# Twelve-token chunks and earlier first products at the head of a fused attention and MoE kernel

## The chip, the cores and the metric

The kernel runs on one core of a Trainium2 chip. The metric is device time in microseconds (us) of one execution. A profiled execution shows a span some 1.8 us shorter than its device time.

## The reference, cut to what matters

```python
# q, k, v: (4, 6080, 256) float32; w_in (256, 2048); w_out (2048, 256)
qn = q / (norm(q, axis=1) + 1e-6);  kn = k / (norm(k, axis=1) + 1e-6)   # norms over the 6080 tokens
s = kn.transpose(0, 2, 1) @ qn / tau                                    # 256 x 256 for each batch
a = softmax(s, axis=-1)
x = v @ a
out = gelu_tanh(x @ w_in) @ w_out
```

The kernel multiplies `a` into `w_in` first (`aw`), so that each block of 512 tokens of v needs one product with `aw` (`hp`), a gelu (`g`) and one product with `w_out` (`yp`). Batch 0's `aw` must exist before that loop begins. The attention of batch 1 is worked on inside the loop of batch 0, and so on.

## The kernel before: the parts that matter

The head, batch 0 (cut):

```python
first_chunks = chunks_of([6, 6, 5, 6, 6, 6, 4, 4, 2, 2], 2)   # tokens per partition; chunk 2 also takes the last 64 tokens
...
for n, ch in enumerate(first_chunks):        # cast q and k to bf16 (DVE), square (ACT), G += k.T q (PE), column sums (PE)
    ...
    stage_chunk(n + 4)                       # next loads, into a free buffer of four
...
for fs in range(D // 512):                   # w_in in four pieces, cast by the load: GpSimd's queue
    nc.gpsimd.dma_start(out=win_bf[:, :, fs * 512 : fs * 512 + 512], in_=...)
load_v(1)
...                                          # w_out in two halves
load_qk(1, 0)                                # batch 1's first chunk of q and k, same queue
load_v(2)
...
T = turned(Gs)
for jc in range(2):
    nc.scalar.activation(eT[:, jc, :], T[:, jc, :], AF.Exp, scale=r[:, jc : jc + 1])
...                                          # v's first block turned on PE
rsinv = row_sums(eT)
...                                          # eight products eT x w_in, scaled by rsinv into aw
```

The loop, what the argument touches (cut):

```python
def attention_steps(b, aw_next):             # one step between two hp groups
    for n in range(10):
        if n % 5 == 0 and (b, n // 5) not in loaded_of:
            load_qk(b, n // 5)
        ...
        yield
    for n, ch in enumerate(later_chunks):
        load_qk(b, n + 2)                    # two chunks ahead of their use
        ...
for blk in range(n_blocks):
    vT = vT_of.pop(nb)
    turn_v(nb + 2)                           # four DMA transposes on SP, vT <- vb, for block nb + 2
    load_v(nb + 3)
    ...
```

## Time and profile before

757.6 us, the median of three runs. The stages of the profiled execution, read from the order of time (starts in us):

| last cast of q, k | root (norms) | T | first hp of the loop | first hp of block 2 | span |
|---|---|---|---|---|---|
| 35.44 | 37.19 | 38.77 | 41.52 | 67.00 | 755.3 |

In the order of time of PE's products (start, length, line, what; in brackets the idle time before it and what is named as ending it) around the start of block 2:

```profile
66.24 0.38 PE L141 MATMUL G<-qkb 128*128 128x256 bf16 x2
67.00 1.02 PE L536 MATMUL hp<-vT,aw 128*128 128x512 bf16 x4 [0.38 <-ACT g L540]
```

PE waits 0.38 us here. The name in brackets is a gelu. But hp also reads vT, and vT of block 2 is written by the transposes that SP issues in this line of its own order of time:

```profile
55.15 10.65 SPq L294 DMA_TRANSPOSE vT<-vb  x8
```

By the landing records of the trace, the fourth of these (the last one for block 2) landed at 66.75, 0.25 us before hp began. The length of an issue in that line is not the time to landing: the fourth was issued at 59.40.

### The profile page before, as it was taken

To read this page: it belongs to the slowest core of one execution; us is meant where nothing else is said; L and a number is where in the kernel's file an instruction comes from. 1 tells how busy PE (TensorE), PEld (TensorE's weight loads), DVE (VectorE), ACT (ScalarE), POOL (GpSimd) and SP (SyncE) were. 2 spreads that over 40 slices of the span, in tenths; PEclk is the share of its full clock that TensorE was granted. 3 is DMA by queue.
4 is the path that set the end of the run, shared out by engine and by line. 5 is a ranking of instruction groups with operands and counts; after the bars stand their busy time and mean duration, and the time that the engine had idled before them with its cause. 6 is when DMAs were issued, how large, how long until landed. Compare 5 with 4: busy or idle time off the path is not lost.

```text
span 755.3 us, 12358 instructions
## 1 busy us (share of the span) xinstructions
PE 738.0 (98%) x5272; PEld 504.6 (67%) x5272; DVE 278.3 (37%) x485; ACT 420.3 (56%) x412; POOL 70.0 (9%) x127
## 2 busy tenths in 40 slices
PE   4899999999999999999999999999999999999998
PEld 3556666667666666666666666666767666666666
DVE  3645545454402545553421455454441011011011
ACT  5775555556455555555555555555545655555552
POOL 0231010001021111001031000100101000000000
PEclk9999999999999999999999999999999999999999
DMA  9999957115149678313449385621512633322111
GB/s 351 357 194 180 189 87 154 53 43 83 43 103 214 133 133 137 65 43 66 101 94 221 80 130 101 125 80 47 82 43 78 111 79 76 69 74 53 41 57 56
DMA packets 80759, 83.59 MB, mean 111 GB/s; under 512 B 55488, under 2 KB 60224, under 8 KB 80704
## 3 DMA queue, kind: packets, MB, share of 16 engines
q0 software_dynamic: 17648, 32.97, 27.0%
q1 hardware_dynamic: 62752, 48.98, 24.6%
q8 instruction: 41, 0.67, 0.4%
q10 hardware_dynamic: 304, 0.85, 0.3%
q14 instruction: 14, 0.11, 0.1%
HBM read 78.91 MB, written 24.90 MB: 137 GB/s over the span
## 4 chain that ended last, share of the span: by engine, by line
PE 95%; DMA 3%; DVE 0%; ACT 0%; SPq 0%; issue 0%; DVEq 0%
PE yp L463 44%; PE hp L536 44%; PE G L141 5%; DMA st<-in_k_dram 3%; PE ps L201 2%; PE cols L153 1%; PE T L179 0%; PE yp L567 0%; PE idle L137 0%; SPq L80 0%; DVE qkb L242 0%; ACT g L540 0%; PE ps L348 0%; ACT eT L328 0%; DVE Gs L171 0%
## 5 line engine op out<-in xcount | busy, mean ns | idle before, releaser
L540 ACT ACTIVATE g<-hp 128x1024 bf16<-128x1024 f32 (+1 forms) x384 | 389.8, 1015 | 308.6 <-PE hp L536 308.5
L463 PE MATMUL yp<-wout_bf,g 128*128 128x256 bf16 x3024 | 392.0, 273 | 0.0
L536 PE MATMUL hp<-vT,aw 128*128 128x512 bf16 (+1 forms) x1536 | 390.8, 377 | 0.4 <-ACT g L540 0.4
L463 PEld LDWEIGHTS <-g 128*128 128x128 bf16 x3024 | 295.9, 98 | 113.4
L536 PEld LDWEIGHTS <-aw 128*128 128x128 bf16 x1536 | 149.9, 98 | 105.0 <-issue 1.3
L480 DVE COPY ysb<-yp 128x512 f32<-128x512 f32 (+1 forms) x95 | 64.9, 683 | 403.1 <-PE yp L463 403.1
L404 DVE TENSOR_TENSOR acc<-acc,sq 128x512 f32<-128x512 f32 (+1 forms) x141 | 97.5, 692 | 4.8
L141 PE MATMUL G<-qkb 128*128 128x256 bf16 (+1 forms) x384 | 69.8, 282 | 12.8 <-DVE qkb L242 12.8
L403 DVE TENSOR_TENSOR sq<-qkb 128x512 bf16<-128x512 bf16 (+1 forms) x141 | 58.7, 417 | 0.0
L141 PEld LDWEIGHTS <-qkb 128*128 128x128 bf16 (+1 forms) x384 | 37.8, 101 | 21.5 <-DVE qkb L242 15.0
L280 POOL DMA_DIRECT2D vb<-in_v_dram x47 | 25.5, 544 | 142.7 <-DMA vT<-vb 122.8
L210 DVE TENSOR_SCALAR aw<-ps,rsinv 128x512 bf16<-128x512 f32 x30 | 22.4, 749 | 27.0 <-PE ps L201 26.7
L247 ACT ACTIVATE sqb<-st 128x3072 bf16<-128x3072 f32 (+3 forms) x9 | 20.4, 2287 | 11.6 <-DMA st<-in_k_dram 11.6
L80 POOL DMA_DIRECT2D qkb<-in_q_dram x24 | 13.0, 542 | 148.7 <-PE hp L536 82.4
L242 DVE CAST qkb<-st 128x3072 bf16<-128x3072 f32 (+4 forms) x11 | 14.5, 1326 | 15.4 <-DMA st<-in_k_dram 15.3
L201 PE MATMUL ps<-win_bf,eT 128*128 128x512 bf16 x60 | 17.7, 379 | 0.0
L414 POOL TENSOR_TENSOR r<-r,half 128x4 f32<-128x4 f32 x3 | 3.1, 1044 | 141.7 <-DVE r L413 141.7
L80 POOL DMA_DIRECT2D qkb<-in_k_dram x24 | 13.1, 544 | 4.1 <-DMA qkb<-in_q_dram 2.3
L520 POOL COPY g<-gr 128x1024 bf16<-128x1024 bf16 x2 | 2.1, 1040 | 105.3 <-PE yp L463 105.3
L439 DVE RECIPROCAL den<-den 128x256 f32<-128x256 f32 x6 | 10.5, 1753 | 0.2
L554 POOL COPY gr<-g 128x1024 bf16<-128x1024 bf16 x2 | 2.1, 1036 | 87.6 <-ACT g L540 87.6
L137 PE MATMUL idle<-filler 128*128 128x512 bf16 x36 | 9.5, 391 | 0.0
(65 smaller groups left out, 85.1 us busy)
## 6 DMA issues: line engine op xcount, KB each, us to landing
out_dram<-ysb SPq DMA_DIRECT2D x44, 512.0 KB, 2.9
vb<-in_v_dram POOLq DMA_DIRECT2D x43, 256.0 KB, 8.6
qkb<-in_q_dram POOLq DMA_DIRECT2D x21, 384.0 KB, 6.6
qkb<-in_k_dram POOLq DMA_DIRECT2D x21, 384.0 KB, 8.7
st<-in_q_dram SPq DMA_DIRECT2D x5, 768.0 KB, 9.5
st<-in_k_dram SPq DMA_DIRECT2D x4, 768.0 KB, 11.3
vT<-vb SPq DMA_TRANSPOSE x184, 3.5
out_dram<-ysb SPq DMA_DIRECT2D x4, 384.0 KB, 4.0
```

The source lines that it names most:

```text
L80: engines[x].dma_start(out=dst[:, x, 0:size, :], in_=src[b, s0 * 128 : (s0 + size) * 128, :].rearrange("(p s) c -> p s c", s=size))
L141: nc.tensor.matmul(G[:, ic, :], lhsT=qk[:rows, 1, s, ic * 128 : ic * 128 + 128], rhs=qk[:rows, 0, s, :], start=first and ic == 0, stop=las ...
L201: nc.tensor.matmul(ps, lhsT=eT[:, jc, ic * 128 : ic * 128 + 128], rhs=win_bf[:, jc, fs * 512 : fs * 512 + 512], start=jc == 0, stop=jc == 1)
L210: nc.vector.tensor_scalar_mul(dst, ps, scale)
L247: nc.scalar.activation(sqb[:rows, :, lo:hi], st[:rows, :, lo:hi], AF.Square)
L280: nc.gpsimd.dma_start(out=t[:, 0:n, :], in_=v_rows[r0 : r0 + n * 128, :].rearrange("(p s) c -> p s c", s=n))
L403: nc.vector.tensor_mul(sq[:rows], flat, flat)
L404: nc.vector.tensor_add(acc[:rows], acc[:rows], sq[:rows])
L463: nc.tensor.matmul(yp[:rows, at, :], lhsT=g[:, fc, s * 128 : s * 128 + rows], rhs=wout_bf[:, fc, :], start=fc == 0, stop=fc == FC - 1)
L480: nc.vector.tensor_copy(ysb[:, s0 : s + 1, :], yp[:, 0 : s + 1 - s0, :])
L536: nc.tensor.matmul(hp[:, j, :cols], lhsT=aw[:, cc, fc * 128 : fc * 128 + 128], rhs=vT[:, cc, :cols], start=cc == 0, stop=cc == 1)
L540: nc.scalar.activation(g[:, 2 * i : 2 * i + 2, :cols], hp[:, :, :cols], AF.Gelu_apprx_tanh)
```

## The change

Its intent: load batch 0's first 24 tokens per partition as rows of 12 KB of q and of k alone, each in a whole buffer, with fewer transfers; square the last chunk on ACT alone; turn v's first block while the norms are worked out; begin the first weight products when half of the exponentials are there. On GpSimd's queue the last two pieces of w_in become one, and v's block 2 is asked for ahead of batch 1's first q and k. The core of the diff, cuts marked:

```diff
-    first_chunks = chunks_of([6, 6, 5, 6, 6, 6, 4, 4, 2, 2], 2)
+    first_chunks = chunks_of([12, 12, 5, 6, 4, 4, 2, 2], 2)
 ...
+    def halves(pool, tag, dtype, size, most=SMAX):   # q and k in a tile each where a chunk has over 6 tokens
 ...
-    for fs in range(D // 512):
-        nc.gpsimd.dma_start(out=win_bf[:, :, fs * 512 : fs * 512 + 512], ...)
+    for c0, c1 in ((0, 512), (512, 1024), (1024, D)):
+        nc.gpsimd.dma_start(out=win_bf[:, :, c0:c1], in_=win_v[:, :, c0:c1])
     load_v(1)
 ...
+    load_v(2)
     load_qk(1, 0)
-    load_v(2)
 ...
-    keep_clock(5)
+    ...                                   # the eight transposes of v's first block on PE
+    keep_clock(1, pY, "y")
     T = turned(Gs)
+    keep_clock(1, pY, "y")
 ...
+    first_aw(0, 0)                        # needs the first half of the exponentials only
+    first_aw(1, 0)
     rsinv = row_sums(eT)
+    first_aw(0, 1)
+    first_aw(1, 1)
 ...
```

More of the change, by code (lines that the diff above doesn't have):

```diff
@@ L80, in load_chunk @@
             engines[x].dma_start(
-                out=dst[:, x, 0:size, :],
+                out=dst[x][:, 0:size, :],
                 in_=src[b, s0 * 128 : (s0 + size) * 128, :].rearrange("(p s) c -> p s c", s=size))
@@ L84, in load_chunk @@
             for x, src in enumerate((q, k)):
-                engines[x].dma_start(out=dst[:REM, x, size, :], in_=src[b, S_ALL * 128 : N, :])
+                engines[x].dma_start(out=dst[x][:REM, size, :], in_=src[b, S_ALL * 128 : N, :])
     def slots_of(chunk):
@@ L91 @@
     n_all = S_ALL + 1
-    first_chunks = chunks_of([6, 6, 5, 6, 6, 6, 4, 4, 2, 2], 2)
-    TAIL, SHARED = 6, 8
-    fillers = [0, 0, 5, 5, 6, 7, 4, 3, 1, 0]
+    first_chunks = chunks_of([12, 12, 5, 6, 4, 4, 2, 2], 2)
+    TAIL, SHARED = 4, 6
+    fillers = [0, 0, 5, 7, 4, 3, 1, 0]
     staged = []
+    def halves(pool, tag, dtype, size, most=SMAX):
+        tiles = [pool.tile([128, 2, most, 256], dtype, tag=tag, name=tag)
+                 for _ in range(1 if size <= most else 2)]
+        if len(tiles) == 1:
+            return [tiles[0][:, x] for x in range(2)], tiles[0]
+        return [t.rearrange("p a b c -> p (a b) c") for t in tiles], None
     def stage_chunk(n):
         if n < len(first_chunks):
+            _, size, rem = first_chunks[n]
             if n < SHARED:
-                st = stage.tile([128, 2, SMAX, 256], FP32, tag="st", name="st")
+                st, whole = halves(stage, "st", FP32, size)
             else:
-                st = staged[n - 2][:, :, first_chunks[n - 2][1] + first_chunks[n - 2][2] :, :]
+                _, size, rem = first_chunks[n - 2]
+                whole = staged[n - 2][1][:, :, size + rem :, :]
+                st = [whole[:, x] for x in range(2)]
             load_chunk((nc.sync, nc.scalar if n < 1 else nc.sync), st, 0, first_chunks[n])
-            staged.append(st)
-    for n in range(4):
+            staged.append((st, whole))
+    for n in range(2):
         stage_chunk(n)
@@ L131, with keep_clock @@
     wout_v = moe_w_out.rearrange("(t p) d -> p t d", p=128)
-    def keep_clock(n):
+    def keep_clock(n, pool=pH, tag="h"):
         for _ in range(n):
-            idle = pH.tile([128, 2, 512], FP32, tag="h", name="idle")
-            nc.tensor.matmul(idle[:, 0, :], lhsT=filler[:, 0:128], rhs=filler, start=True, stop=True)
+            idle = pool.tile([128, 2, 512] if pool is pH else [128, 512], FP32, tag=tag, name="idle")
+            nc.tensor.matmul(idle[:, 0, :] if pool is pH else idle, lhsT=filler[:, 0:128], rhs=filler, start=True, stop=True)
     def gram(G, qk, s, rows, first, last):
@@ L142, in gram @@
                 G[:, ic, :],
-                lhsT=qk[:rows, 1, s, ic * 128 : ic * 128 + 128],
-                rhs=qk[:rows, 0, s, :],
+                lhsT=qk[1][:rows, s, ic * 128 : ic * 128 + 128],
+                rhs=qk[0][:rows, s, :],
                 start=first and ic == 0,
@@ L154, in col_sums @@
                 cols[:, m : m + 1],
-                lhsT=x[:, m // 2, m % 2 * 128 : m % 2 * 128 + 128],
+                lhsT=x[m // 2][:, m % 2 * 128 : m % 2 * 128 + 128],
                 rhs=ones,
@@ L220, in sums_of @@
         for m, x in enumerate(parts):
-            col_sums(cols, x, ones_bf[: x.shape[0], :], summed == 0, last and m == len(parts) - 1)
+            col_sums(cols, x, ones_bf[: x[0].shape[0], :], summed == 0, last and m == len(parts) - 1)
             summed += 1
@@ L227, in pairs_of @@
         h = size // 2
-        pair = prp.tile([128, 2, SMAX // 2, 256], BF16, tag="pair", name="pair")
-        nc.vector.tensor_add(pair[:, :, 0:h], sqb[:, :, 0:h], sqb[:, :, h : 2 * h])
-        parts = [pair[:, :, s, :] for s in range(h)]
+        pair, whole = halves(prp, "pair", BF16, h, SMAX // 2)
+        for x in range(2):
+            nc.vector.tensor_add(pair[x][:, 0:h], sqb[x][:, 0:h], sqb[x][:, h : 2 * h])
+        parts = [[y[:, s, :] for y in pair] for s in range(h)]
         if size % 2:
-            parts.append(sqb[:, :, size - 1, :])
+            parts.append([y[:, size - 1, :] for y in sqb])
+        if first_chunks[n][2]:
+            parts.append([y[:REM, size, :] for y in sqb])
         sums_of(parts, False)
@@ L236 @@
     for n, ch in enumerate(first_chunks):
-        st = staged[n]
+        st, whole = staged[n]
         size = ch[1]
-        qkb = qkp.tile([128, 2, SMAX, 256], BF16, tag="qk", name="qkb")
-        sqb = sqp.tile([128, 2, SMAX, 256], BF16, tag="sq", name="sqb")
+        qkb, qk_whole = halves(qkp, "qk", BF16, size)
+        sqb, sq_whole = halves(sqp, "sq", BF16, size)
         for lo, hi, rows in [(0, size, 128)] + ([(size, size + 1, REM)] if ch[2] else []):
-            nc.vector.tensor_copy(qkb[:rows, :, lo:hi], st[:rows, :, lo:hi])
-            if n >= n_chunks - 2:
-                nc.scalar.activation(sqb[:, 1, lo:hi], st[:, 1, lo:hi], AF.Square)
-                nc.vector.tensor_mul(sqb[:, 0, lo:hi], qkb[:, 0, lo:hi], qkb[:, 0, lo:hi])
-            else:
-                nc.scalar.activation(sqb[:rows, :, lo:hi], st[:rows, :, lo:hi], AF.Square)
+            if whole is None:
+                todo = [(qkb[x][:, lo:hi], sqb[x][:, lo:hi], st[x][:, lo:hi]) for x in range(2)]
+            else:
+                todo = [(y[:rows, :, lo:hi] for y in (qk_whole, sq_whole, whole))]
+            for to, sq, x in todo:
+                nc.vector.tensor_copy(to, x)
+                if n != n_chunks - 2:
+                    nc.scalar.activation(sq, x, AF.Square)
+            if n == n_chunks - 2:
+                nc.scalar.activation(sqb[1][:, lo:hi], st[1][:, lo:hi], AF.Square)
+                nc.vector.tensor_mul(sqb[0][:, lo:hi], qkb[0][:, lo:hi], qkb[0][:, lo:hi])
         keep_clock(fillers[n])
@@ L254 @@
             waiting = None
-        if n < TAIL:
+        if n < 2:
+            pairs_of(n, sqb)
+        elif n < TAIL:
             waiting = (n, sqb)
         else:
-            sums_of([sqb[:rows, :, s, :] for s, rows in slots_of(ch)], n == n_chunks - 1)
-        stage_chunk(n + 4)
+            sums_of([[y[:rows, s, :] for y in sqb] for s, rows in slots_of(ch)], n == n_chunks - 1)
+        for x in ((2, 3) if n == 0 else (4, 5) if n == 1 else (n + 4,)):
+            stage_chunk(x)
         if n == n_chunks - 3:
-            nc.gpsimd.tensor_copy(gate[:, 0:1], st[0:1, 1, 0, 0:1])
+            nc.gpsimd.tensor_copy(gate[:, 0:1], st[1][0:1, 0, 0:1])
     v0 = stage.tile([128, 2, SMAX, 256], FP32, tag="st", name="v0")
@@ L304, in load_qk @@
             t = qkp.tile([128, 2, SMAX, 256], BF16, tag="qk", name="qkb")
-            load_chunk((nc.gpsimd, nc.gpsimd), t, b, later_chunks[n])
-            loaded_of[b, n] = t
-    for fs in range(D // 512):
-        nc.gpsimd.dma_start(out=win_bf[:, :, fs * 512 : fs * 512 + 512],
-                            in_=win_v[:, :, fs * 512 : fs * 512 + 512])
+            views = [t[:, x] for x in range(2)]
+            load_chunk((nc.gpsimd, nc.gpsimd), views, b, later_chunks[n])
+            loaded_of[b, n] = views, t
+    for c0, c1 in ((0, 512), (512, 1024), (1024, D)):
+        nc.gpsimd.dma_start(out=win_bf[:, :, c0:c1], in_=win_v[:, :, c0:c1])
     load_v(1)
@@ L323 @@
     Gs = scaled(G, r)
-    keep_clock(5)
+    vps = []
+    for cc in range(2):
+        p = pH.tile([128, 2, 512], FP32, tag="h", name="vps")[:, 0, :]
+        for s in range(4):
+            nc.tensor.matmul(p[:, s * 128 : s * 128 + 128],
+                             lhsT=v0[:, s, cc * 128 : cc * 128 + 128],
+                             rhs=ident, is_transpose=True)
+        vps.append(p)
+    keep_clock(1, pY, "y")
     T = turned(Gs)
+    keep_clock(1, pY, "y")
+    vT0 = vts.tile([128, 2, 512], BF16, tag="vT", name="vT")
@@ L326 @@
+    nc.vector.tensor_copy(vT0[:, 0, :], vps[0])
     eT = smx.tile([128, 2, 256], BF16, tag="eT", name="eT")
+    aw = awp.tile([128, 2, D], BF16, tag="aw", name="aw")
     for jc in range(2):
         nc.scalar.activation(eT[:, jc, :], T[:, jc, :], AF.Exp, scale=r[:, jc : jc + 1])
-    vT0 = vts.tile([128, 2, 512], BF16, tag="vT", name="vT")
-    for cc in range(2):
-        vps = pH.tile([128, 2, 512], FP32, tag="h", name="vps")[:, 0, :]
-        for s in range(4):
-            nc.tensor.matmul(vps[:, s * 128 : s * 128 + 128],
-                             lhsT=v0[:, s, cc * 128 : cc * 128 + 128],
-                             rhs=ident, is_transpose=True)
-        if cc == 0:
-            nc.vector.tensor_copy(vT0[:, cc, :], vps)
-        else:
-            nc.scalar.activation(vT0[:, cc, :], vps, AF.Copy)
@@ L340 @@
-    rsinv = row_sums(eT)
-    aw = awp.tile([128, 2, D], BF16, tag="aw", name="aw")
-    for lo, pool, tag in ((0, pY, "y"), (256, pA, "a")):
-        for ic in range(2):
-            ps = pool.tile([128, 512], FP32, tag=tag, name="ps")
-            for jc in range(2):
-                nc.tensor.matmul(
-                    ps[:, 0:256],
-                    lhsT=eT[:, jc, ic * 128 : ic * 128 + 128],
-                    rhs=win_bf[:, jc, lo : lo + 256],
-                    start=jc == 0, stop=jc == 1)
-            dst, scale = aw[:, ic, lo : lo + 256], rsinv[:, ic : ic + 1]
-            if lo == 0 and ic == 1:
-                nc.scalar.activation(dst, ps[:, 0:256], AF.Copy, scale=scale)
-            else:
-                nc.vector.tensor_scalar_mul(dst, ps[:, 0:256], scale)
+    nc.scalar.activation(vT0[:, 1, :], vps[1], AF.Copy)
@@ new lines, with first_aw @@
+    firsts = []
+    def first_aw(n, jc, pool=pY, tag="y"):
+        if jc == 0:
+            firsts.append(pool.tile([128, 512], FP32, tag=tag, name="ps"))
+        nc.tensor.matmul(
+            firsts[n][:, 0:256],
+            lhsT=eT[:, jc, n % 2 * 128 : n % 2 * 128 + 128],
+            rhs=win_bf[:, jc, n // 2 * 256 : n // 2 * 256 + 256],
+            start=jc == 0, stop=jc == 1)
+    first_aw(0, 0)
+    first_aw(1, 0)
+    rsinv = row_sums(eT)
+    first_aw(0, 1)
+    first_aw(1, 1)
+    for n in (2, 3):
+        first_aw(n, 0, pA, "a")
+        first_aw(n, 1)
@@ L358 @@
+    for n in range(4):
+        ic, lo = n % 2, n // 2 * 256
+        dst, scale = aw[:, ic, lo : lo + 256], rsinv[:, ic : ic + 1]
+        if n == 1:
+            nc.scalar.activation(dst, firsts[n][:, 0:256], AF.Copy, scale=scale)
+        else:
+            nc.vector.tensor_scalar_mul(dst, firsts[n][:, 0:256], scale)
     nc.scalar.activation(dummy, ones_f, AF.Gelu_apprx_tanh)
@@ L393, in attention_steps @@
             load_qk(b, n + 2)
-            qk = loaded_of.pop((b, n))
+            qk, whole = loaded_of.pop((b, n))
             for s, rows in slots_of(ch):
@@ L397, in attention_steps @@
                 gram(G, qk, s, rows, first, last)
-                flat = qk[:rows, :, s, :]
+                flat = whole[:rows, :, s, :]
                 if first:
@@ L410, in attention_steps @@
         cols = pA.tile([128, 512], FP32, tag="a", name="cols")
-        col_sums(cols, acc, ones_f, True, True)
+        col_sums(cols, [acc[:, x] for x in range(2)], ones_f, True, True)
         r = smx.tile([128, 4], FP32, tag="r", name="r")
```

## The prediction

> **What bounds the kernel now.** I read the page first, then the chain of waits, then the windows of the first 50 us, then the order of time there. The page says that TensorE sets the pace and that the change can only touch the head:
>
> ```profile
> PE 738.0 (98%) x5272; PEld 504.6 (67%) x5272; DVE 278.3 (37%) x485; ACT 420.3 (56%) x412; POOL 70.0 (9%) x127
> PE   4899999999999999999999999999999999999998
> DMA  9999957115149678313449385621512633322111
> PE 95%; DMA 3%; DVE 0%; ACT 0%; SPq 0%; issue 0%; DVEq 0%
> ```
>
> The reader is to see that PE is busy in 38 of 40 slices and that the chain that ended last is PE for 95% and DMA for 3%. One slice is 18.9 us; DMA is at nine tenths in the first two and never so steadily again. From 41.5 us to the end (714 us) the windows show 709.9 us of PE busy, and the waits between 41 and 80 us list one of 0.4 us for PE, those after it none. The change edits only what precedes the loop, plus the order of a few loads at its start. Everything it can win lies in the first 41.5 us, 5.5% of the span.
>
> In that head the loads come first. The windows (columns: stretch and length, busy time of PE, PEld, DVE, ACT, POOL, clock, DMA share, GB/s):
>
> ```profile
> 4.00:6.00 2.00, 0.00 (x0) 0.00 (x0) 0.00 (x0) 0.00 (x0) 0.00 (x0) 1.00 0.99 418
> 14.00:16.00 2.00, 2.00 (x21) 1.35 (x19) 1.86 (x3) 1.87 (x1) 0.00 (x0) 1.00 0.98 356
> 30.00:32.00 2.00, 2.00 (x26) 1.44 (x24) 2.00 (x3) 2.00 (x2) 0.00 (x0) 1.00 1.02 388
> 34.00:36.00 2.00, 2.00 (x31) 1.71 (x30) 1.68 (x3) 1.78 (x3) 2.00 (x4) 1.00 0.71 169
> ```
>
> The reader is to see a DMA share of about 1 from 4 us to 34 us: there is no gap in the loads to close, only a rate to raise. Then the chain in order of time (start, length, what):
>
> ```profile
> 27.60 1.77 DVE qkb L242
> ...
> 36.40 0.46 PE G L141 x4
> 36.85 0.31 PE cols L153 x8
> ...
> 37.19 0.18 ACT r L320
> ...
> 38.14 0.49 DVE Gs L171
> ...
> 38.77 0.75 PE T L179 x4
> ...
> 39.54 0.85 ACT eT L328 x2
> ...
> 40.44 0.23 PE rs L188 x3
> 40.66 0.90 PE ps L348 x8
> 41.56 0.56 PE hp L536 x2
> ```
>
> The last chunk of q and k lands at 35.43; its cast ends at 36.18, just as PE's backlog with fillers runs out (36.22), so landing and backlog are balanced. After that come the column sums, norms, scaling, turning, two exponentials, row sums and eight weight products, each waiting for the last, up to the first product of the loop at 41.52.
>
> **What the Trainium skill says.** "DMA: Bandwidth & Descriptors", section "Why small descriptors are slow (HBM only)", gives a fixed overhead of about 3 cycles per packet inside the DMA engine. The packet records agree in kind: undisturbed packets of 1, 2, 4, 5 and 6 KB took 46, 84, 160, 200 and 234 ns, about 8 ns plus 38 ns per KB. The same page, section "Issuing engines are not separate DMA queues", says that SP, ACT and GpSimd feed the same 16 engines; the trace agrees, the windows stay near 420 GB/s with k on ACT's queue or on SP's. "TensorE: Matmul & The Clock Gate", Part 1, says that an idle PE runs at half rate until about 3.4 us of activity. Here the first 12 G products took 2.74 us and those at 20.39 took 1.48, although the clock line reads 1.00 throughout. "ScalarE: Activation LUTs" states 0.833 ns per element for any function; 128x2048 in 1904 ns against 128x512 in 624 gives 0.833.
>
> **The change part by part.**
>
> *Rows of 12 KB.* The chunks of 6, 6, 5, 6, 6, 6, 4, 4, 2, 2 tokens per partition become 12, 12, 5, 6, 4, 4, 2, 2: four chunks of six turn into two of twelve. Each engine then moves 32 packets of about 8 + 12x38 = 464 ns instead of 64 of 234: 14.98 us become 14.85. At the measured mean of about 238 after 15 us the gain is up to 0.25. Four fewer transfers drop as many 9 ns completion packets on each engine. I choose **0.2 us** earlier landing. It is small because 6 KB rows already run at 16x6144/234 = 420 GB/s.
>
> *Later start of work.* The first chunk pair now lands when 3.1 MB are in, not 1.6: 16 packets of 464 ns in place of 16 of 234, so at about 7.1 + 3.7 = 10.8 us. DVE casts q and k (1.76 each), until 14.4; PE starts there, not at 8.9, and does 24 cold G products in about 5.5 us. ACT squares the four tiles of six (2.76 each) until about 21.9. This is off the path if it has caught up by the last big chunk, which lands at about 27: chunk 2 lands near 21.8, is cast by about 24.8, and ACT is free near 25. It has, by some 2 us. Cost on the path: **0**.
>
> *Buffers.* Both first chunks take all four stage buffers, so chunk 2 is issued when ACT has squared the first q, at 10.8 + 2.76 = 13.6 us; chunk 1's k is in transfer until about 17.6. Chunk 3 goes out at 16.4, chunks 4 and 5 at about 19.2 and 22, while chunk 2 and then chunk 3 run to 21 and 25. The DMA stays fed by 2 us or more each time. Cost: **0**.
>
> *Last chunk's squares.* Before: cast 0.74, then a DVE product of 0.42, ended 36.74, 1.31 us after the landing. Now ACT squares q and k of the last chunk together, 1024 elements: 624 + 512x0.833 = 1.05 us from the landing. G products end about as the squares do, so sums follow some **0.15 us** earlier; the order on PE takes back the rest of the 0.26.
>
> *Transposes of v before T.* The eight (1.04 us) move from the time of the exponentials, where they were free, to the wait for the norms, where five fillers of 1.24 us were. Both places lie beside other work: **0**. They need v's first block by about 36.8.
>
> *First products by halves.* Before, from T's start at 38.77 to the first product of the loop took 2.75 us. Now two of eight weight products run before the second exponential has ended. T 0.75, two exponentials to 1.61 (by the distances above), row sums to 1.87, six products of 0.11 to 2.53; the scaled copy needs 0.05 + 0.17 (reciprocal) + 0.43 after the row sums, also 2.52. The loop starts 2.55 after T: **0.2 us** saved. ACT's second scaled copy still waits behind the v copy (0.60), and ended only 0.11 us after the loop's first product before, so I trim this to 0.15.
>
> *Weights in three pieces, v2 ahead of batch 1.* The last 1 MB of w_in lands as one. Before, waits on its four pieces ended at 40.63, 41.89 and 44.12 (second to fourth). The products of the third piece ran first at 44.12, over 2 us after it was there; now they wait for the whole last MB. Fewer, longer packets bring it in by my estimate at 43.2, PE now asks at about 43.6: no wait, narrowly. Batch 1's first q and k come about 1.4 us later, near 55, and are asked for at 57.67 - 0.5: **0**.
>
> Sum: 0.2 + 0.15 + 0.15 = 0.5 us; fewer instructions and waits at the seams may give 0.2 to 0.3 more. From the median of 757.6 I take **756.9 us**.
>
> **The rivals.** (1) *Nothing moves*: the slowest DMA engine sets each landing. The records show an instruction fetch of 16 KB that took 1105 ns at 24.58 us; the last 2 KB packets ended at 34.88 on one engine, while the middle ones started the last round near 33.6. If that engine lags more, the 0.2 us vanish: 757.2 to 757.6. If the fetch falls after the loads, up to 1.1 us more are won: 755.8. (2) *A wait on w_in or on v takes the place of the products*: margins of 0.4 us and less. It costs 0.3 to 0.6 us and ends level, 757.4. (3) *The loads run dry* because all buffers sit in two chunks: ACT's squares would have to be over 2 us later than worked out; each us of gap is a us of time, 758 to 759. Against it speaks that ACT was 2.4 us idle and more per chunk before. (4) *PE comes late out of its cold start*: 5 us later, with 48 products at once. If it is still behind at 27 us, 0.5 to 1 us are lost. (5) *The loop slides otherwise*: other DMA timing changes waits of PE; it has only 0.4 us of waits there, so little to win and little seen to lose.
>
> **Range and chances.** The runs before span 757.37 to 758.07, so 0.35 us either way is noise. Best case, 1.1 us from the fetch and 0.8 of the sum: 755.7. Worst likely case, rival 2 or 4 with no gain from the rows: 758.1. Range 755.7 to 758.1. A 2% change is 15.2 us, over a third of the whole head; no part reaches 2 us. Chances: faster 0.005, same 0.99, slower 0.005.
>
> **What would show it right or wrong.** Rows: packets of 12288 bytes near 464 ns, DMA share near 1 from 4 to 34 us, last landing at 35.1 to 35.3. Start: first cast near 10.8, PE from 14.4, but no wait of PE longer than before after the chunk of six. Squares: under 1.65 us from the last landing to the root, 1.76 before. Products: 2.6 us from T to the loop's first product, 2.75 before, and the loop at about 41.0. A wait of the first products or of T for v or w_in would show rival 2; a DMA share well below 1 between 14 and 26 us rival 3. The prediction is wrong if the loop starts on time and the span still moves by over 1.5 us, for then the loop itself, 714 us of PE, has changed.

## The result, and the profile after

Median 758.0 us (757.31 to 758.32, six runs); the kernel before, in the same rounds, 757.59 (757.25 to 758.07). The ratio is 1.0003, 95% interval 0.999 to 1.0016. Here and below a ratio is the mean time of one kernel's fast runs over that of the other's of the same rounds, so not quite the ratio of the medians quoted. The page of the kernel after, the lines that answer to those of before:

```profile
PE 730.0 (97%) x5175; PEld 503.6 (67%) x5262; DVE 277.7 (37%) x486; ACT 420.4 (56%) x412; POOL 69.2 (9%) x126
DMA  8999957225139778313549377721512633322111
PE 90%; issue 5%; DMA 3%; POOL 1%; SPq 0%; ACT 0%; DVE 0%; POOLq 0%; ACTq 0%
PE yp L500 43%; PE hp L573 41%; PE G L153 4%; DMA vb<-in_v_dram 2%; DMA vT<-vb 2%; PE ps L213 1%; SPq L318 0%; POOL win_bf L334 0%; PE cols L165 0%; PE yp L604 0%; POOL wout_bf L337 0%; PE T L191 0%; ACT g L577 0%; POOL vb L304 0%; POOL filler L129 0%
```

(PE's smaller count is mostly records missing from the trace: 1457 hp products are recorded, 1536 weight loads of them.) The chain's DMA share is again 3%, but it is other DMA: before it was k's load in the head, now it is a block of v and its transposes. The chain in order of time (start, length, what) shows where they stand:

```profile
37.79 14.19 DMA vb<-in_v_dram
...
55.91 11.91 DMA vT<-vb
67.82 0.14 issue
67.95 1.02 PE hp L573 x4
```

The reader is to see that nothing of the head's computing is on this chain. The path runs from the issue of v's block 2 at 37.79 over its landing at 51.98 and four transposes to the first hp of block 2. It is not free of the head's loads: GpSimd asks for w_in only when the k of the third-last chunk is there, and in all fourteen profiles it did so 0.17 to 0.18 us after that landing. In the kernel after that was 0.26 us earlier than before (32.58, not 32.84), and the transposes still landed 1.07 us later. The waits of PE from 41 us to the end (total, times, longest):

```profile
PE hp L573 <- DMA vT<-vb: 1.2, 1, 1.2
PE ps L213 <- DMA win_bf<-in_moe_w_in_dram: 0.5, 1, 0.5
PE hp L573 <- DVE aw L394: 0.2, 1, 0.2
```

Two new waits: one for w_in's last 1 MB, one for the transposes. Stage by stage:

| start, us | last cast | root | T | first hp | third piece's products | first hp of block 2 | span |
|---|---|---|---|---|---|---|---|
| before | 35.44 | 37.19 | 38.77 | 41.52 | 44.12 | 67.00 | 755.3 |
| after | 35.22 | 36.83 | 38.16 | 40.91 | 44.21 | 67.95 | 756.2 |

The head won 0.61 us and the loop began at 40.91. All of it was gone by 44.2: the last 1 MB of w_in landed at 44.17, and the products that read it came 3.30 us after the first hp instead of 2.60. At block 2 another 0.86 us were lost. From block 2 on nothing differs: from its first gelu to the end of the span there are 687.2 us in the kernel before, 687.1 in the kernel after, and one or the other in each variant below.

### The profile page after: what moved, and what is told of

Its sections match the earlier page's. It is cut to its first block, busy times and chain, and to the rows that moved or that the text cites. A ratio compares the mean times of both kernels' runs of the same rounds, so it can differ in the third digit from the quotient of the medians.

```text
span 756.2 us, 12239 instructions
## 1 busy us (share of the span) xinstructions
PE 730.0 (97%) x5175; PEld 503.6 (67%) x5262; DVE 277.7 (37%) x486; ACT 420.4 (56%) x412; POOL 69.2 (9%) x126
## 3 DMA queue, kind: packets, MB, share of 16 engines
q1 hardware_dynamic: 62176, 48.20, 24.3%
## 4 chain that ended last, share of the span: by engine, by line
PE 90%; issue 5%; DMA 3%; POOL 1%; SPq 0%; ACT 0%; DVE 0%; POOLq 0%; ACTq 0%
PE yp L500 43%; PE hp L573 41%; PE G L153 4%; DMA vb<-in_v_dram 2%; DMA vT<-vb 2%; PE ps L213 1%; SPq L318 0%; POOL win_bf L334 0%; PE cols L165 0%; PE yp L604 0%; POOL wout_bf L337 0%; PE T L191 0%; ACT g L577 0%; POOL vb L304 0%; POOL filler L129 0%
## 5 line engine op out<-in xcount | busy, mean ns | idle before, releaser
L573 PE MATMUL hp<-vT,aw 128*128 128x512 bf16 (+1 forms) x1457 | 385.0, 377 | 5.4 <-DMA vT<-vb 1.2
L153 PE MATMUL G<-qkb 128*128 128x256 bf16 (+1 forms) x288 | 55.0, 273 | 0.0
L153 PEld LDWEIGHTS <-qkb 128*128 128x128 bf16 (+1 forms) x288 | 27.9, 98 | 3.8 <-issue 0.6
L153 PE MATMUL G<-qk 128*128 128x256 bf16 (+1 forms) x96 | 14.2, 307 | 15.5 <-DVE qk L262 15.4
L264 ACT ACTIVATE sq<-st 128x3072 bf16<-128x3072 f32 (+4 forms) x10 | 21.2, 2160 | 11.8 <-DMA st<-in_q_dram 8.4
L153 PEld LDWEIGHTS <-qk 128*128 128x128 bf16 (+1 forms) x96 | 10.1, 110 | 19.4 <-DVE qk L262 16.8
L262 DVE CAST qk<-st 128x3072 bf16<-128x3072 f32 (+4 forms) x11 | 14.3, 1323 | 13.9 <-DMA st<-in_q_dram 10.1
L213 PE MATMUL ps<-win_bf,eT 128*128 128x512 bf16 x54 | 16.4, 379 | 0.5 <-DMA win_bf<-in_moe_w_in_dram 0.5
## 6 DMA issues: line engine op xcount, KB each, us to landing
st<-in_q_dram SPq DMA_DIRECT2D x2, 1536.0 KB, 11.9
```

The source lines that it names most:

```text
L153: nc.tensor.matmul(G[:, ic, :], lhsT=qk[1][:rows, s, ic * 128 : ic * 128 + 128], rhs=qk[0][:rows, s, :], start=first and ic == 0, stop=las ...
L213: nc.tensor.matmul(ps, lhsT=eT[:, jc, ic * 128 : ic * 128 + 128], rhs=win_bf[:, jc, fs * 512 : fs * 512 + 512], start=jc == 0, stop=jc == 1)
L264: nc.scalar.activation(sq, x, AF.Square)
L573: nc.tensor.matmul(hp[:, j, :cols], lhsT=aw[:, cc, fc * 128 : fc * 128 + 128], rhs=vT[:, cc, :cols], start=cc == 0, stop=cc == 1)
```

## The experiments

**Theory.** The first hp of block 2 waits for the transposes of v's block 2. They share the DMA engines with a stream of loads on GpSimd's queue (w_in, w_out, batch 1's q and k, blocks of v) that is busy without a break from 35 us on, and they land only when that stream pauses. This pins the rest of the program, already in the kernel before. **Rivals**: the wait for w_in alone is the loss; the transposes are slow of themselves; the head's gain was luck. In each diff below, "late third chunk" stands for

```diff
-            load_qk(b, n + 2)
+            for m in ((), (2, 3))[n] if b == 1 and n < 2 else (n + 2,):
+                load_qk(b, m)
```

so that batch 1's third chunk is asked for at 64.8 to 66.4 us in the profiles, not at 53.5 to 55.6. It is used only after the first two chunks.

### What pins the loop

First four runs, on one chip; the kernel before beside them had a median of 757.51 (756.92 to 757.75).

**a_pieces4**: after, with w_in in four pieces.

```diff
-    for c0, c1 in ((0, 512), (512, 1024), (1024, D)):
+    for c0, c1 in ((0, 512), (512, 1024), (1024, 1536), (1536, D)):
```

> Kernel after, w_in's last 1 MB again as two pieces. Theory (stream): the first hp of block 2 waits for the transposes of v's block 2, which land only when the loads of batch 1 issued by GpSimd have drained; so the 0.7 us wait of PE for w_in at 43.5 us goes (products of the third piece at 43.6 instead of 44.21), PE comes to block 2 at about 66.0 instead of 66.7, and waits there until about 67.5 to 67.9 as before: time as after, 757.7 to 758.1. Rival (w_in): the wait for w_in is what was lost, nothing pins block 2: 757.2 to 757.4, 0.6 under after.

**a_delay**: after, with the late third chunk.

> Kernel after, but batch 1's third chunk of q and k is asked for with its fourth, one chunk later (about 69 us instead of 54), so it isn't ahead of the transposes. Theory (stream): the transposes of block 2 land by about 64.5, PE starts block 2 as it comes, at about 66.7 instead of 67.9: 756.7 to 756.9. Rival (w_in): nothing changes at block 2, 757.8 to 758.1. Rival (transposes are slow of themselves, whatever runs beside them): they still land at about 67, 757.3 to 758.

**a_pieces4_delay**: after, with both.

> Both of the above. Theory (stream): the two savings add only together: block 2 starts at about 66.0, 1.9 us before that of after and 0.9 before that of the kernel before: 756.0 to 756.4. Rival (w_in): 757.2 to 757.4, as with the four pieces alone.

**a_order**: after, with the old order of two loads.

```diff
-    load_v(2)
     load_qk(1, 0)
+    load_v(2)
```

> Kernel after, with v's block 2 asked for behind batch 1's first q and k again. Theory (stream): the transposes start at about 55.5 instead of 52 and have landed when the stream has drained, which they take less from: the fourth lands at about 66.8 to 67.2 instead of 67.8, time 757.2 to 757.6. If the later drain comes from the slower stream between 36 and 40 us alone (some 0.4 us), the order changes nothing: 757.8 to 758.1.

| | median (lowest to highest) | ratio to before | fourth transpose landed | first hp of block 2 |
|---|---|---|---|---|
| a_pieces4 | 757.96 (757.69 to 758.17) | 1.0009 | 68.02 | 68.15 |
| a_order | 757.61 (757.44 to 757.93) | 1.0004 | 67.56 | 67.70 |
| a_delay | 756.57 (756.20 to 757.18) | 0.9991 | 64.47 | 66.57 |
| a_pieces4_delay | 756.53 (756.32 to 756.86) | 0.9990 | 64.23 | 66.33 |

The theory holds. With four pieces PE no longer waited for w_in, and nothing was won: the wait stood at block 2 instead. (In this one profile the loop also began late, at 42.09 instead of 40.91, so the profile alone doesn't say that the pieces took the wait away; the five times say that it would have made no difference.) Its line in the waits of PE:

```profile
PE hp L573 <- DMA vT<-vb: 1.0, 1, 1.0
```

With one chunk asked for later and nothing else changed (a_pieces4 against a_pieces4_delay), the runs are 1.4 us apart and don't overlap. In the order of time of a_delay, PE's block 2 now begins as PE comes, with no wait in brackets:

```profile
66.35 0.38 PE L153 MATMUL G<-qkb 128*128 128x256 bf16 x2
66.57 1.03 PE L574 MATMUL hp<-vT,aw 128*128 128x512 bf16 x4
```

This rules out transposes that are slow of themselves as the reason for a landing near 67. (A part of their time is not touched by the late chunk: from the first issue to the first packet it took 3.8 to 4.0 us in all fourteen profiles. What holds them so long is open.) Two expectations missed. a_order's fourth transpose should have landed at 66.8 to 67.2 and landed at 67.56, 0.26 us before that of after; the order is taken up again below. And four pieces on top of the late chunk should have brought another 0.6 us and brought none in the median. In the profile of a_delay the loop began at 41.63 rather than 40.91, so w_in had landed (43.65) before PE asked for it; the wait for w_in costs only where the head came early.

### Was the kernel before pinned too, and what are the parts of the change worth?

Kernel before beside these: 757.30 (757.10 to 757.93).

**b_delay**: before, with the late third chunk.

> Kernel before, with only batch 1's third chunk asked for one chunk later. Theory (stream): before too waited at block 2 for the transposes, by little (PE there at 66.6, first hp at 67.0): 757.1 to 757.3 and no wait of hp at block 2, the transposes landed by 64.5. If before was not pinned, no change: 757.5.

**b_chunks_delay**: that, with the chunks of the kernel after.

```diff
-    first_chunks = chunks_of([6, 6, 5, 6, 6, 6, 4, 4, 2, 2], 2)
+    first_chunks = chunks_of([12, 12, 5, 6, 4, 4, 2, 2], 2)     # and what belongs to it in the change
```

> As b_delay, with the chunks of the kernel after (12, 12, 5, 6, 4, 4, 2, 2, and the last chunk's squares on ACT) but its attention part and its order and pieces of loads as before. With nothing pinned at block 2, this shows what the head is worth: last landing 0.2 earlier, squares 0.13 shorter, so 0.3 to 0.6 under b_delay, 756.6 to 756.9. If the earlier loop start of the kernel after was only its run's luck: no difference to b_delay within 0.15.

**b_products_delay**: b_delay with the attention part of the kernel after.

```diff
-    keep_clock(5)
+    ...                                   # v's transposes ahead of T, as in the change
+    first_aw(0, 0)
+    first_aw(1, 0)
     rsinv = row_sums(eT)
```

> As b_delay, with the attention part of the kernel after (v's transposes before T, two first products at half the exponentials) and chunks as before. As I predicted: from T to the loop's first product 2.6 us instead of 2.75, 0.15 under b_delay. As the trace of after suggests (2.75 us there too, as the row sums, the reciprocal and the scaled copy set it, all behind the second exponential): 2.75 and no difference to b_delay beyond 0.1.

**b_again**: the kernel before, one look.

> Kernel before unchanged, for a second profile of its head: how far the last landing (35.43) and the loop's start (41.52) move between runs. If the head is steady: 41.4 to 41.6. If it moves as in the variants of after (40.9 to 42.1): outside that, while block 2 starts at 67.0 all the same.

| | median (lowest to highest) | ratio to before | last cast | T to first hp | first hp of block 2 |
|---|---|---|---|---|---|
| b_delay | 756.50 (756.30 to 757.85) | 0.9991 | 35.19 | 2.75 | 66.20 |
| b_chunks_delay | 756.89 (756.64 to 757.14) | 0.9994 | 35.87 | 2.75 | 66.93 |
| b_products_delay | 756.63 (756.34 to 756.91) | 0.9991 | 35.19 | 2.75 | 66.22 |
| b_again | 756.82 (one run) | | 35.42 | 2.76 | 66.72 |

The kernel before was pinned: b_delay has no wait of PE after 41 us and is 0.8 us under its neighbours in the median, more than the 0.2 to 0.4 that I expected. (One of its five runs, 757.85, lies among theirs, and the interval, 0.9979 to 1.0004, holds 1; what shows the pin is the trace.) Its head also came 0.25 us earlier than the first profile's, which is run-to-run scatter. In b_again the loop began at 41.50, as in the first profile, but the fourth transpose landed at 66.47 instead of 66.75, and block 2 moved with it, to 66.72. In all seven profiles without the late chunk, hp of block 2 began 0.1 to 0.3 us after that landing.

The first products by halves are worth nothing: T to first hp is 2.75 us with them as without. The chain in order of time of b_products_delay shows why:

```profile
38.53 0.75 PE T L179 x4
...
39.84 0.39 PE ps L350 x2
40.23 0.21 PE rs L188 x4
...
40.46 0.18 DVE rsinv L194
...
40.74 0.50 DVE aw L370
...
41.28 1.04 PE hp L550 x4
```

After the row sums (end 40.44) come DVE's reciprocal and its scaled copy, and hp 0.84 us later. Before, PE's eight products ended at just about the time when these two were done; taking two of them off PE leaves the path over DVE as long as it was.

The chunks of 12 are not worth the 0.2 us either: with nothing pinned, b_chunks_delay is 0.4 us over b_delay in the median, not 0.3 to 0.6 under it; why is told under *Chunks* below.

### The order, the chunks in a pinned kernel, and the remainder

Kernel before beside these: 757.12 (756.96 to 758.47).

**b_order**: before, with one line moved.

```diff
+    load_v(2)
     load_qk(1, 0)
-    load_v(2)
```

> Kernel before, with only the order of two loads changed: v's block 2 ahead of batch 1's first q and k. Theory (order): the transposes of block 2 go out at about 52 instead of 55 and take their turns between the loads, which drain later; the fourth lands at about 67.0 to 67.5 instead of 66.5 to 66.75, so 0.3 to 0.7 over before. Rival (head): the order does nothing, and what came later in the kernel after is the stream's own late start: 66.5 to 66.8, within 0.15 of before.

**b_chunks**: before, with the chunks of the kernel after.

> Kernel before, with only the chunks of the kernel after (12, 12, 5, 6, 4, 4, 2, 2 and the last squares on ACT); attention part, order and pieces of loads as before. Theory: the last landing comes either near 35.2 or near 35.9 as in the six runs of such chunks, not steadily earlier; block 2 is pinned by the transposes, the fourth lands at 66.6 to 67.2, time within 0.3 of before. If the rows of 12 KB were worth the 0.2 us that I had predicted: a last landing of 35.2 and block 2 still at 67.0.

**a_pieces4_delay_rem** and **b_delay_rem**: the last 64 tokens of batch 0 loaded at the start, on ACT's queue.

```diff
-        if rem:
+        if rem and b > 0:
 ...
+    rest0 = const.tile([REM, 2, 1, 256], FP32)
+    for x, src in enumerate((q, k)):
+        nc.scalar.dma_start(out=rest0[:, x, 0, :], in_=src[0, S_ALL * 128 : N, :])
```

> Kernel after with four pieces of w_in and the late third chunk, and the 64 rows of 1 KB of batch 0's remainder (q and k) loaded at the start into a tile of their own instead of behind chunk 2. Theory (remainder): the stretch in which packets took twice their time (about 1 us on each engine between 20 and 23 us) goes with it, the last landing is at about 34.5 to 34.9 instead of 35.2 to 35.9, and the program, pinned by nothing, is 0.4 to 0.9 faster than without: 755.7 to 756.1. Rival: the stretch belongs to the change from the first chunks to those loaded into freed buffers, whatever the row size; then it stays, 756.5.

> The same move of the remainder in the kernel before with the late third chunk (chunks of 6). Theory (remainder): the stretch of slow packets at 13 to 15 us, 0.54 us on each engine, goes; last landing 34.7 to 34.9 instead of 35.2, 755.9 to 756.2. With both gone, rows of 12 KB against 6 KB show their worth alone: the run with chunks of 12 lands 0.2 us earlier than this one if they are worth what their packets' durations say.

| | median (lowest to highest) | ratio to before | last cast | fourth transpose landed |
|---|---|---|---|---|
| b_order | 757.88 (757.04 to 758.27) | 1.0005 | 35.82 | 67.88 |
| b_chunks | 757.42 (756.76 to 757.68) | 1.0001 | 35.09 | 66.61 |
| a_pieces4_delay_rem | 756.98 (755.99 to 757.10) | 0.9990 | 35.17 | 64.77 |
| b_delay_rem | 756.41 (756.31 to 756.45) | 0.9986 | 35.31 | 63.59 |

*Order.* b_order's fourth transpose landed at 67.88, as in the kernel after and 1.1 us later than in before; its wait at block 2:

```profile
PE hp L536 <- DMA vT<-vb: 1.1, 1, 1.1
```

The stream's landing records tell how. From the landing of v's block 3 to that of batch 1's third k take 9.40, 9.40, 9.79 and 9.46 us in the four kernels with the old order and no late chunk (before, b_again, b_chunks, a_order), and 10.27, 10.24 and 10.30 in the three with the new (after, a_pieces4, b_order). The transposes then go out at 52 instead of 55, their packets start to move at 56.0 to 56.3 instead of 58.5 to 59.7, and they take turns with the loads: 0.75 us more for the stream. After its end the fourth transpose landed 0.63 to 0.72 us later with the new order and 0.94 to 1.09 with the old, so 0.3 come back: net about 0.45 us. The rest of the 1.07 us between after and before is in the stream up to v's block 3, which landed between 55.3 and 57.1 over all fourteen profiles, with either order; I can't tell how much of that comes from the three pieces and how much is scatter. The times alone don't resolve the order either: b_order is above its neighbours in the median, but the interval (0.9992 to 1.0017) holds 1, and a_order's ratio is like that of after.

*Chunks.* In the pinned kernel the new chunks change nothing that the times show, as expected. The last cast began at 35.09 to 35.30 in four of the seven profiles with chunks of 12 (the two with the moved remainder left out) and at 35.87 to 35.99 in three; with chunks of 6 at 35.19 to 35.44 in four of five, at 35.82 in one. The means are 35.5 and 35.4. Two things that the traces record explain this scatter; both stood among the prediction's rivals.

The first is rival 1, the slowest DMA engine. A load tells its landing by 16 records, one for each engine. In every profile an instruction fetch of 16 KB takes one engine 1.07 to 1.11 us, starting between 24.3 and 28.8 us. Until then the last record of a load comes at most 0.53 us after the last but one; from the first load that lands after the fetch on, it comes 0.6 to 1.7 us after it, and so one engine alone sets the last landing of q and k. By the middle engine (the eighth record) that load landed at 33.50 to 33.95 with chunks of 6 and at 33.68 to 34.08 with chunks of 12. The kernel after has the 34.08, 0.32 us later than the 33.76 of before. It landed 0.23 us earlier all the same (35.09, not 35.32), because its last engine was only 0.63 us behind, not 1.43. No run moves the fetch; that it causes the lag is read from the order in time alone.

The second is rival 4, PE's late start. From 25 to 36.5 us PE was busy for 9.4 to 10.1 of the 11.5 us with chunks of 6 and for 10.6 to 11.5 with chunks of 12. In three of the eight profiles with chunks of 12 (a_pieces4, b_chunks_delay and a_pieces4_delay_rem), and in none of the six others, the granted clock fell to 0.50 between 20.7 and 24.3 us. The same stretch in a_pieces4_delay_rem and in after (PE busy first, clock third from the end):

```profile
21.00:24.00 3.00, 3.00 (x15) 2.14 (x16) 2.77 (x3) 2.58 (x2) 0.00 (x0) 0.50 1.02 419
21.00:24.00 3.00, 3.00 (x45) 2.74 (x44) 2.86 (x3) 2.41 (x2) 0.00 (x0) 1.00 1.00 307
```

PE then worked without a pause from 23.8 to 37.5, and the root followed this backlog, at 37.72 to 37.85, 1.73 to 2.56 us after the last cast; in the other five it came 1.61 to 1.66 after. So in the profile of b_chunks_delay the root stood 0.94 us behind that of b_delay (37.85, 36.91).

*Remainder.* This expectation was half right. The slow packets go where the remainder goes: the time above the fastest packet of the same size, summed and divided by 16 engines, was 0.55 us between 13 and 15 us in before and 1.00 between 20 and 23 in after; with the remainder moved to the start it was 0.35 and 0.50, at 7 to 10 and at 11 to 15 us, and the old places were clean. But the last landing hardly moved: from 35.17 to 35.05 with chunks of 12 (a_pieces4_delay, a_pieces4_delay_rem) and from 35.07 to 35.19 with chunks of 6 (b_delay, b_delay_rem). It is that of the slowest engine; the middle one's went from 33.83 to 33.58 and from 33.55 to 33.57. With both slow stretches gone, 12 KB and 6 KB rows stand at 33.58 and 33.57: no gain from the rows. The time of a_pieces4_delay_rem is clouded by the clock: three of its five runs had a mean of 0.997 or 0.998 and took 756.98 to 757.10, the two at 0.999 and 1.000 took 756.37 and 755.99, against the 755.7 to 756.1 expected.

*The best version* is b_delay_rem, 756.41 us, the only one of twelve whose interval (0.9974 to 0.9999) lies below 1 against the kernel before; among twelve, one so close to 1 may be chance. It is 0.14% ahead of the kernel before; the kernel after was not run beside it. By the medians all of it is the late third chunk: 0.71 us under its neighbours, where b_delay alone, on another chip, was 0.80 under its own. Whatever the chunks or the products may be worth would have to show on top of this version.

## Why the prediction was right or wrong

The time, 758.0, lies in the stated range and near its upper end. The sign was wrong: I said 0.7 us faster, the median came out 0.4 slower, and within the noise it is no change. That the time lies so near is in part luck: some steps went as worked out, some gains didn't come, and what did come was lost at two waits. By its steps:

- **The rate of the loads**: the packets behaved as worked out (460 ns for 12 KB, 464 predicted). Their gain over 6 KB, 32 x (2 x 234 - 460) ns = 0.26 us for each engine, was given back by the slow stretch at the remainder, 0.45 us longer than before. The step "I choose 0.2 us earlier landing" failed on the average of the profiles. That this one profile shows 0.22 is luck: its middle engine was 0.32 us later, and its slowest one less far behind. Rival 1 is what decided it, but it cut both ways.
- **The late start and the buffers**: right in this profile. The first cast began at 11.04 (10.8), PE at 14.52 (14.4), the issues stood at 13.83, 16.48, 19.18 and 21.79 (13.6, 16.4, 19.2, 22). PE's first 24 products took 5.10 us (5.5). "Cost on the path: 0" holds here, but not in the three profiles with the clock at 0.50, where rival 4 came true. (The prediction reads the clock line's 1.00 as full clock throughout; the trace of before has no clock record until 16.4 us, so the line says nothing of the first products.) The loads did not run dry: in the windows of the kernel after the DMA share is about 1, although between 20 and 22 us, at the remainder, it moved less (second-last column share, last GB/s):

```profile
14.00:16.00 2.00, 1.48 (x8) 1.05 (x9) 1.33 (x2) 2.00 (x1) 0.00 (x0) 1.00 0.99 424
20.00:22.00 2.00, 1.36 (x20) 1.17 (x17) 1.86 (x3) 1.76 (x1) 0.00 (x0) 1.00 1.13 293
30.00:32.00 2.00, 2.00 (x28) 1.41 (x25) 2.00 (x3) 1.85 (x1) 0.00 (x0) 1.00 1.03 396
```

- **The last chunk's squares**: right, 1.61 us from the last cast to the root instead of 1.75, and 1.61 to 1.66 in the five profiles where PE was not behind.
- **Products by halves**: wrong, 2.75 us and not 2.6. I had set the reciprocal and the scaled copy to end with PE's last product, and sized them too small: from the row sums to hp 0.84 us where I counted 0.65. In b_products_delay the two took 0.68 (I had 0.60), and the time between one engine and the next came to 0.16 (I had 0.05).
- **The loop's start**: 40.91 as predicted ("about 41.0"), but partly by the lucky landing, and partly by a term that I did not have: root to T fell from 1.58 to 1.33, as DVE's addition took 0.17 us instead of 0.42. The shorter distance came in four of the seven profiles with chunks of 12 and in none of those with chunks of 6; its cause is open.
- **w_in in three pieces**: rival 2, named and under-sized. The last 1 MB landed at 44.17, not at 43.2, and held PE up for 0.70 us, not 0.3 to 0.6. As it turned out it cost nothing of its own, for PE would have waited at block 2.
- **"Weights in three pieces, v2 ahead of batch 1: 0"** is the step that failed. I asked when batch 1's first q and k were needed and found room, and they did land in time. I did not ask what the earlier arrival of v's block 2 would set off: transposes that compete with the loads behind which they then wait. By the landings this cost some 0.45 us of the 1.07 by which the fourth transpose came later; the times don't resolve it.
- **"It has only 0.4 us of waits there, so little to win and little seen to lose"** (rival 5) failed with it. That wait of 0.4 us was the tip of the pin. It stood under the name of a gelu. A wait that short at the one place where a transfer must have landed says that the transfer is just in time, and then whatever comes earlier upstream of PE is lost there.

How the stream and the transposes share the engines fits the Trainium skill, "DMA: Bandwidth & Descriptors", section "Queues, rings and completion order": each DMA engine goes round its queues packet by packet. In the kernel before, between 60 and 62 us, a load's packet took about 240 ns and a transpose's about 30; taking turns, the transposes should get 30 of 270, a ninth of the time: by this estimate that of 1.8 engines of 16. The time of their packets came to that of 2.1 to 2.2 engines while the loads ran, and of over 22 (packets overlap) when the loads were done. This rough agreement is all that was shown for the mechanism (and it takes a record of the trace for such a packet); what was shown by experiment is that the loads ahead of them decide when the transposes land.

## What to carry to other kernels

Before shortening a head, look for the first place behind it where the bounding engine waits for a transfer that does not hang on what was shortened: what is won upstream ends there. A wait of a few tenths can be such a pin, and the name that the profile gives it can be that of another engine. The cheap remedy is to take from the busy DMA queue, ahead of the urgent transfer, whatever isn't needed for a while.

## What the Trainium skill lacked or had wrong

- "DMA: Bandwidth & Descriptors", "DMA Transpose (X-bar)": says nothing of the time of transposes issued beside a busy stream of loads. Here a transpose issued at 55.91 us landed 11.9 us later, and from the end of the loads on they landed about 0.3 us apart. From the first one's issue to its first packet 3.8 to 4.0 us passed in every profile.
- The same page, "Why small descriptors are slow (HBM only)": explains a cost per packet, and the fastest packets here agree in kind (about 8 ns plus 38 ns per KB). It does not have that 128 packets of 1 KB to 64 partitions slow down the larger packets around them: those of 6 KB that followed in the kernel before took up to 507 ns instead of 234.
- The same page, "Specifications", gives some 358 GB/s as the limit of HBM for a core, half of what two cores share; its section "Bandwidth" says that this holds with both cores streaming, and has a measured 425 GB/s for a core alone. This program uses one core, and the kernel after shows 418 to 436 GB/s in the windows from 4 to 14 us, so the first figure alone would mislead here.
- I found no page that gives the time that one engine needs to follow another through a chain of small steps of a kernel; here row sums, reciprocal, scaled copy and product left 0.02 to 0.11 us between each two.
